# A one-element exponential after the gelus of seven of the nine first MLP stages, and fills dealt 12, 10, 9 instead of 14, 9, 8

## The chip, the cores and the metric

The kernel runs on one core of a Trainium2 chip. The metric is the device time of one execution in microseconds (us), median over several runs. A profile is one execution, and its span (first to last instruction) is some 2 us shorter than the time. All runs told of here count as fast, with a granted TensorE clock of 0.998 to 1.000 but for four long ones.

Names: PE is TensorE, ACT is ScalarE, DVE is VectorE, POOL is GpSimd. "L223" is line 223 of the kernel. The changed kernel has a few lines more, so that line 223 of before (exp of the scores) is line 228 after it, and 232 in two of the experiments.

## The reference

Forgetting attention over 8 batches, 8 heads, 576 tokens, 64 per head, and then an MLP with the tanh form of gelu over all 4608 tokens:

```python
scores = scale * q @ k.T + (cum[:, None] - cum[None, :])   # cum: running sum of log f
attn   = softmax(causal(scores)) @ v
x      = attn as (4608, 512)
h      = x @ w_in                       # 512 -> 2048
out    = gelu_tanh(h) @ w_out           # 2048 -> 512
```

Two functions of ScalarE alternate, exp for the softmax and gelu for the MLP, and the engine loads a table at each change (seven loads for the gelus and seven for the exps of the scores in the steady part of the trace).

## The kernel before

The heads are worked in groups of four, `i` = 0 to 15, and the tokens in nine chunks of 512, `c`. A loop step does the first MLP stage of chunk `c` (eight pieces, a gelu behind each) and then a pair of head groups. In between it strews *fills*: `out_part(c, n)` issues `n` steps of the second MLP stage, so that PE has work while ACT turns scores into exponentials.

```python
def scores(i, r, groups=((0, 1, 2, 3),)):
    ...
        tiles = {g: psS.tile([128, 2, 512], FP32, name="ps_s", tag="s") for ...}   # both buffers of psS
        ...  matmuls of the four heads into the two tiles
        for g, t in tiles.items():
            nc.scalar.activation(p[:, 2 * g:2 * g + 2, off:off + n], t[:, :, 0:n], AF.Exp, scale=scale)   # L223

def mlp_in(c, prs):
    ...
        nc.scalar.activation(gT[c % 2][:, 2 * pr:2 * pr + 2, :], ph, AF.Gelu_apprx_tanh)   # L332

def pair(i, j, c):
    D, V = ...                           # D: denominators, V: attention output
    beside(i, 0, c, [D(j), 14])          # scores of round 0, D(j), masks of the round, 14 fills
    beside(i, 1, c, [V(j, 0), 9])
    beside(i, 2, c, [V(j, 1), 8])
    ...

run(FRONT)                               # an opening table of words (it holds chunks 0 and 1): S/H scores, F/f fills,
for c in range(2, NCH):                  # J/I first MLP stage, B idle matmuls, D, V, ...
    out_part(c - 1, CH)
    ...
    for pr in range(2, NP):
        mlp_in(c, (pr,))
    if c + 1 < B:
        out_part(c, 6)
        pair(2 * c + 3, 2 * c + 2, c)
```

A block of scores takes both buffers of `psS`; the next block can only start when both exps have read them. How many fills lie between two blocks decides whether PE gets there before ACT is done.

The softmax here doesn't subtract the row's maximum and nothing guards it: scores larger than these inputs give would overflow.

Of the kernel before, what the change touches and what calls it, by code (L numbers as in the profile page):

```python
# [8 lines left out]
FP32 = mybir.dt.float32  # L9
BF16 = mybir.dt.bfloat16  # L10
AF = mybir.ActivationFunctionType
# [5 lines left out]
def kernel(  # L17
# [10 lines left out]
    nc = tc.nc  # L28

    B, H, S, D = q.shape  # L30
# [44 lines left out]
        LP.3 B.1.256 vw.1.0 WI.1@LU.4 W H.1.1.1 WI.3 B.2.256 WI.2 H.1.0.0 M.1.0.1 D.0.0 M.1.0.0 H.0.1.1 V.0.0.0 H.0.1.0 B.2.256 M.0.1 H.1.1.0 V.0.1.0  # L75
        D.1.0 H.0.3.0 B.2.128 V.1.0.0 LX.1.1 H.0.3.1 V.1.1.0 m.0.3.2 H.1.3.0 m.0.3.4 B.1.256 VW.1.1 H.1.3.1 B.4.128 vw.0.1 D.0.1 M.1.3 S.1.2 M.1.1 LK.2
        V.0.1.1 V.0.0.1 WO.0 J.0.1 D.1.1 J.0.0 WO.1@LV.1.1 V.1.1.1 V.1.0.1 J.0.3 WO.2@WI.1 VW.3 J.1.0 WO.3 LK.3 LQ.3 J.1.1 TQ.2 J.1.3 LQ.4
        LX.1.0@WO.2 TK.2 J.0.2 J.1.2 LK.4 F.0.6 TK.3 B.3.256 S.2.0 LK.5 F.0.9 S.2.2 F.0.10 S.2.1 TQ.3 TQ.4 F.0.10 LV.2.0@LK.5 m.2.1 vw.2
        TK.4 S.3.0 f.0.1 M.2.2 CL.2 LQ.5 M.2.0 D.2 f.0.6 S.3.1 m.3.0 F.0.6 V.2.0 S.3.2 TK.5 LK.6 M.3.2 f.0.7 V.2.1 CL.3
        S.4.1 m.3.1 LQ.6 F.0.6 TQ.5 H.4.2.1 D.3 H.4.0.1 LQ.7 VW.4 H.4.0.0 V.3.1 v.3.0 f.0.3 H.4.2.0 CL.4 I.1.0 m.4.1 LV.2.1@LQ.5 I.1.5  # L80
        TQ.6 m.4.2.3 I.1.1 I.1.7 LV.3.0@LQ.7 m.4.2.2 TK.6 M.4.0 I.1.3 I.1.2 I.1.4 I.1.6 F.1.8 S.5.0 F.1.2 F.1.14 S.5.1 D.4 M.5.0 f.1.9
        S.5.2 V.4.0 m.5.2.3 f.1.6 VW.5 V.4.1 CL.5 m.5.2.2 LQ.8 S.6.0 f.1.6 M.5.1 D.5 f.1.4 S.6.1 V.5.1 f.1.7 V.5.0 vw.6 S.6.2
        m.6.1 M.6.2.2 m.6.0 m.6.2.3 LK.7 LK.8 CL.6 LX.3.1@LK.6
    """
# [1 line left out]
    singles = ctx.enter_context(tc.tile_pool(name="singles", bufs=1))  # L86
# [6 lines left out]
    def many(n, shape, dtype, name):  # L93
        return [singles.tile(shape, dtype, name=f"{name}{i}") for i in range(n)]
# [11 lines left out]
    vw = many(2, [128, NT + 1, 4, D], BF16, "vw")  # L106
# [9 lines left out]
    w_bf = singles.tile([128, NQ, NT + 1, 4], BF16, name="w_bf")  # L116
    shift = singles.tile([128, 1], FP32, name="shift")
    idle = singles.tile([128, 512], BF16, name="idle")
    causal = many(2, [128, 128], BF16, "causal")


# [62 lines left out]
    def key_columns(i, key, h, c):  # L184

        b0 = {"low": 0, 0: 1, 1: 3, 2: 5, 3: 7, "high": NB}[key]
        return kT[i % 2][32 * h:32 * h + 32, 64 * b0:64 * b0 + 128, c]

    idle_ps = []

# [6 lines left out]
    def scores(i, r, groups=((0, 1, 2, 3),)):  # L197

        qq, p = qT[i % 2], pt[i % 2]
        if i < 2:  # L200
            off, n = split_rounds[r]
            todo = [(key, col - off, q0, nq) for (key, col, q0, nq) in split_pieces[r]]
        else:
            off, n = rounds[r]
            todo = []
            for (key, col, q0, nq) in pieces:
                a, z = max(col, off), min(col + nq, off + n)
                if a < z:
                    todo.append((key, a - off, q0 + a - col, z - a))
        for heads in groups:  # L210
            tiles = {g: psS.tile([128, 2, 512], FP32, name="ps_s", tag="s") for g in sorted({h // 2 for h in heads})}
            for c in range(2):
                for j, (key, c0, q0, nq) in enumerate(todo):
                    for h in heads:
                        nc.tensor.matmul(  # L215
                            tiles[h // 2][:, h % 2, c0:c0 + nq],
                            key_columns(i, key, h, c),
                            qq[32 * h:32 * h + 32, q0:q0 + nq, c],
                            start=(c == 0 and j == 0), stop=(c == 1),
                            skip_group_check=True,  # L220
                        )
            for g, t in tiles.items():
                nc.scalar.activation(p[:, 2 * g:2 * g + 2, off:off + n], t[:, :, 0:n], AF.Exp, scale=scale)  # L223
# [68 lines left out]
    def denominators(i, part=None):  # L292

        def column(h):

            return lambda t: (w_bf[:, i, t, h:h + 1] if t not in (0, LOW) else
                              w_bf[:, i, t, h:h + 1].to_broadcast([128, 32]))

        po = product(i, [(32 * h, column(h), h) for h in range(4)], False, part)
        n = S if part is None else parts[part][1] - parts[part][0]  # L300
        den = den_pool.tile([128, S], FP32, name="den", tag="den")
        nc.vector.transpose(out=den[:, 0:n], in_=po)  # L302
        rec = den_pool.tile([128, S // 32], FP32, name="rec", tag="rec")
        nc.vector.reciprocal(rec[:, 0:n // 32], den[:, 0:n:32])
        rb = den_pool.tile([128, S], FP32, name="rb", tag="rb")
        nc.vector.transpose(out=rb[:, 0:n].rearrange("p (c j) -> p c j", j=32),  # L306
                            in_=rec[:, 0:n // 32].unsqueeze(2).to_broadcast([128, n // 32, 32]))
        rbs[i, part] = rb[:, 0:n]

    def attn_out(i, x, spare=False, part=None):  # L310
        b, u = i // QPB, i % QPB
        po = product(i, [(32 * h, lambda t, h=h: vw[i % 2][:, t, h, x:D:2], h) for h in range(4)], spare, part)
        s0, s1 = (0, S) if part is None else parts[part]
        nc.vector.tensor_mul(xT[:, 2 * u + x, S * b + s0:S * b + s1], po, rbs[i, part])  # L314
# [37 lines left out]
    def mlp_out(c):  # L352

        for n in range(CH // 128):
            r0 = CH * c + 128 * n
            last = c == NCH - 1 and n == CH // 128 - 1
            st = ostage_pool.tile([128, D_MODEL], FP32, name="o_st", tag="o")
            for (m0, m1) in ((0, 384), (384, 512)) if last else ((0, D_MODEL),):
                pso = psM.tile([128, D_MODEL], FP32, name="pso", tag="m")
                for ft in range(N_FT):  # L360
                    cols = 32 if by_columns else 128
                    for c0 in range(0, 128, cols):
                        nc.tensor.matmul(pso[c0:c0 + cols, m0:m1],  # L363
                                         gT[c % 2][:, ft, 128 * n + c0:128 * n + c0 + cols],
                                         w_out_sb[:, ft, m0:m1],
                                         start=(ft == 0), stop=(ft == N_FT - 1), skip_group_check=True)
                    if ft == N_FT - 1:
                        nc.vector.tensor_copy(st[:, m0:m1], pso[:, m0:m1])  # L368
                        eng = nc.scalar if m0 else nc.sync
                        eng.dma_start(out=out[r0:r0 + 128, m0:m1], in_=st[:, m0:m1])  # L370
                    yield
# [61 lines left out]
    def pull(it, n):  # L433
        for _ in range(n):
            if next(it, False) is False:
                return
# [4 lines left out]
    def out_part(c, n, tiled=0):  # L441
        by_columns[:] = [True] * tiled
        pull(fills.setdefault(c, mlp_out(c)), n)
# [5 lines left out]
    def load_values(b, half):  # L449
# [33 lines left out]
        "F": out_part,  # L483
        "f": lambda c, n: out_part(c, n, 1),
        "B": keep_busy,
    }

    def run(table):
# [10 lines left out]
    def beside(i, r, c, todo):  # L499

        if i is not None:
            scores(i, r)
        for n, x in enumerate(todo):
            if isinstance(x, int):
                out_part(c, x, 1)
            else:
                x()
            if n == 0 and i is not None:
                after_scores(i, r)

    def after_scores(i, r):
        mask(i, r)
        if r == 1:
            make_vw(i, nc.gpsimd)
        if r == 2:
            copy_low(i)

    def pair(i, j, c):

        D, V = (lambda q: lambda: denominators(q)), (lambda q, x, spare=False: lambda: attn_out(q, x, spare))  # L520
        beside(i, 0, c, [D(j), 14])
        beside(i, 1, c, [V(j, 0), 9])
        beside(i, 2, c, [V(j, 1), 8])
        if i + 1 < NQ:
            beside(i + 1, 0, c, [D(i), 10])
            beside(i + 1, 1, c, [V(i, 0), 5, V(i, 1), 4])
            scores(i + 1, 2)
            after_scores(i + 1, 2)
        else:
            beside(None, 0, c, [D(i), 10, V(i, 0), V(i, 1, True), 10])  # L530
# [11 lines left out]
    with tc.manual_schedule():  # L542
        setup()
        run(FRONT)
        for c in range(2, NCH):
            out_part(c - 1, CH)
            for pr in range(2):
                mlp_in(c, (pr,))
            if c + 1 < B:
                prepare(2 * c + 3, 2 * c + 4)  # L550
            if c + 2 < B:
                load_v(c + 2)
            for pr in range(2, NP):
                mlp_in(c, (pr,))
            if c + 1 < B:
                out_part(c, 6)
                pair(2 * c + 3, 2 * c + 2, c)
        out_part(NCH - 1, CH)
# [30 lines left out]
```

## Time and profile before

| | before |
|---|---|
| time, median of 6 runs | 343.32 us (342.74 to 343.62) |
| span of the profile | 341.2 us |
| opening, from the idle matmuls at 42.17 us to the first MLP stage of chunk 1 at 68.39 | 26.22 us, PE busy 24.98 |
| chunk 1, the rest of the opening table, 68.39 to 104.36 | 35.97 us, PE busy 35.97 |
| steps c = 2 to 6, 104.36 to 282.42 | 178.06 us, PE busy 177.78 |
| tail (c = 7 and 8), 282.42 to the end | 58.78 us |

The rows come from asking the busy time of each engine in those stretches, which start and end at the same instructions in every kernel here. I call 42.17 to 68.39 the *opening* and 68.39 to 282.42 (214.03 us) the *loop*, though its first 35.97 us belong to the opening table: they are the stage of chunk 1. What is not PE's busy time looks like what a change outside PE can win: 1.24 us in the opening, nothing in chunk 1, and 0.28 us after it.

Rows, in order of time: start, duration, engine, line, operation, count; in brackets the idle time before it and who ended it.

```profile
47.21 2.33 PE L363 MATMUL pso<-w_out_sb,gT 128*128 128x512 bf16 x10
...
64.20 1.14 PE L215 MATMUL ps_s<-qT,kT 32*128 32x64 bf16 x24
...
66.38 0.87 PE L283 MATMUL ps_o<-pt,vw 128*32 128x512 bf16 x24 [0.24 <-ACT pt L223]
...
275.00 0.28 PE L283 MATMUL po<-pt,w_bf 128*1 128x192 bf16 x8 [0.28 <-POOL pt L229]
```

and ACT:

```profile
65.31 1.94 ACT L223 ACTIVATE pt<-ps_s 128x1024 bf16<-128x1024 f32 x2 [0.70 <-PE ps_s L215]
```

From the start of a block of scores at 64.20 to its exps at 65.31 it takes 1.11 us. The row at 275.00 is the last pair's wait for a mask.

### The profile page before, as it was taken

How to read it: one execution, taken by the hardware profiler on the slowest of the kernel's cores; microseconds unless marked ns; L12 is line 12 of the kernel's file. 1: busy time of each engine (PE TensorE's matmuls, PEld its weight loads, DVE VectorE, ACT ScalarE, POOL GpSimd, SP SyncE). 2: the span in 40 equal slices, each digit the busy share in tenths (PEclk: the TensorE clock that was granted, in tenths of full speed). 3: DMA queues.
4: the chain of work that ended last, by engine and by line, in shares of the span. 5: the costliest groups of instructions: out<-in, count | busy, mean ns of one | idle time of the engine just before them, and what ended most of it. 6: DMA issues, size and time to landing. Idle time of an engine off the chain costs nothing.

```text
span 341.2 us, 9416 instructions
## 1 busy us (share of the span) xinstructions
PE 330.1 (97%) x4241; PEld 162.2 (48%) x4241; DVE 132.2 (39%) x206; ACT 191.3 (56%) x194; POOL 110.0 (32%) x155
## 2 busy tenths in 40 slices
PE   3999989999999999999999999999999999999996
PEld 1458834544454445444444444444444544444443
DVE  4785049740455435603452234414430450011011
ACT  4784576676557566656575665665575724502510
POOL 8996551600506224601651055105410410000000
PEclk9999999999999999999999999999999999999999
DMA  7999999670315971491029310920100011011012
GB/s 122 213 214 208 194 230 190 106 171 2 87 46 77 244 159 35 120 200 52 35 67 202 73 66 35 190 51 33 65 31 2 33 52 44 2 61 61 0 39 86
DMA packets 40200, 33.26 MB, mean 97 GB/s; under 512 B 27472, under 2 KB 29776, under 8 KB 40160
## 3 DMA queue, kind: packets, MB, share of 16 engines
q0 software_dynamic: 8848, 16.58, 27.5%
q1 hardware_dynamic: 31168, 16.01, 16.9%
q8 instruction: 33, 0.54, 0.7%
q10 hardware_dynamic: 144, 0.07, 0.1%
q14 instruction: 7, 0.06, 0.1%
HBM read 36.85 MB, written 9.44 MB: 136 GB/s over the span
## 4 chain that ended last, share of the span: by engine, by line
PE 83%; POOL 1%; ACT 1%; issue 1%; POOLq 0%; DVE 0%; ACTq 0%
PE pso L363 35%; PE ps_h L325 32%; PE po L283 8%; PE ps_s L215 7%; ACT pt L223 1%; POOL vw L177 1%; PE ps_o L283 0%; POOL pt L229 0%; POOLq L584 0%; DVE o_st L368 0%; POOLq L229 0%; ACTq L223 0%
## 5 line engine op out<-in xcount | busy, mean ns | idle before, releaser
L363 PE MATMUL pso<-w_out_sb,gT 128*32 128x512 bf16 (+3 forms) x1492 | 134.5, 377 | 0.0
L223 ACT ACTIVATE pt<-ps_s 128x1024 bf16<-128x1024 f32 (+2 forms) x100 | 93.9, 991 | 49.6 <-PE ps_s L215 42.2
L325 PE MATMUL ps_h<-xT,w_in_sb 128*128 128x512 bf16 x512 | 111.9, 379 | 0.0
L332 ACT ACTIVATE gT<-ps_h 128x1024 bf16<-128x1024 f32 x64 | 65.5, 1023 | 64.2 <-PE ps_h L325 64.2
L229 POOL TENSOR_SCALAR_AFFINE_SELECT pt<-pt 128x512 bf16<-128x512 bf16 (+3 forms) x65 | 38.0, 594 | 141.6 <-ACT pt L223 140.8
L363 PEld LDWEIGHTS <-gT 128*32 128x32 bf16 (+1 forms) x1492 | 56.3, 97 | 56.8 <-issue 3.5
L325 PEld LDWEIGHTS <-w_in_sb 128*128 128x128 bf16 x512 | 50.0, 98 | 60.4 <-issue 0.4
L368 DVE COPY o_st<-pso 128x512 f32<-128x512 f32 (+2 forms) x37 | 24.9, 673 | 72.2 <-PE pso L363 71.8
L215 PE MATMUL ps_s<-qT,kT 32*128 32x64 bf16 (+5 forms) x896 | 36.3, 263 | 1.2 <-ACT pt L223 1.2
L302 DVE STREAM_TRANSPOSE den<-po 128x576 f32<-128x576 f32 x14 | 11.0, 783 | 64.5 <-PE po L283 64.5
L314 DVE TENSOR_TENSOR xT<-po,rb 128x576 bf16<-128x576 f32 x26 | 19.7, 757 | 32.7 <-PE po L283 32.6
L177 POOL TENSOR_TENSOR vw<-v_nat,wT 128x1280 bf16<-128x1280 f32 (+1 forms) x13 | 30.0, 2309 | 0.1
L215 PEld LDWEIGHTS <-kT 32*128 32x128 bf16 x896 | 16.6, 93 | 24.8 <-issue 19.4
L160 DVE STREAM_TRANSPOSE kT<-k_c 128x576 f32<-128x576 f32 x16 | 19.9, 1246 | 16.5 <-DMA k_c<-in_k_dram 16.5
L283 PE MATMUL po<-pt,vw 128*32 128x64 bf16 (+4 forms) x624 | 22.4, 278 | 0.0
L160 DVE STREAM_TRANSPOSE qT<-q_c 128x576 f32<-128x576 f32 x16 | 19.9, 1244 | 1.5 <-DMA q_c<-in_q_dram 0.8
L283 PEld LDWEIGHTS <-vw 128*32 128x32 bf16 x672 | 14.2, 97 | 12.2 <-issue 4.1
L131 POOL DMA_DIRECT2D v_nat<-in_v_dram x20 | 15.3, 777 | 3.6 <-DMA w_out_sb<-in_moe_w_out_dram 3.6
L342 PE MATMUL ps_h<-xT,w_in_sb 128*128 128x256 bf16 x128 | 14.5, 273 | 0.0
L342 PEld LDWEIGHTS <-w_in_sb 128*128 128x128 bf16 x128 | 12.3, 98 | 1.7
L306 DVE STREAM_TRANSPOSE rb<-rec 128x576 f32<-128x576 f32 (+2 forms) x18 | 12.8, 712 | 0.6
L283 PE MATMUL po<-pt,w_bf 128*32 128x512 bf16 (+3 forms) x336 | 12.3, 278 | 0.3 <-POOL pt L229 0.3
(60 smaller groups left out, 120.3 us busy)
## 6 DMA issues: line engine op xcount, KB each, us to landing
out_dram<-o_st SPq DMA_DIRECT2D x35, 256.0 KB, 2.0
k_c<-in_k_dram POOLq DMA_DIRECT2D x16, 288.0 KB, 6.2
q_c<-in_q_dram POOLq DMA_DIRECT2D x16, 288.0 KB, 7.2
v_nat<-in_v_dram SPq DMA_DIRECT2D x16, 256.0 KB, 8.6
w_in_sb<-in_moe_w_in_dram POOLq DMA_DIRECT2D x4, 512.0 KB, 9.6
w_out_sb<-in_moe_w_out_dram POOLq DMA_DIRECT2D x4, 512.0 KB, 7.6
v_nat<-in_v_dram SPq DMA_DIRECT2D x16, 128.0 KB, 3.1
v_nat<-in_v_dram POOLq DMA_DIRECT2D x13, 128.0 KB, 7.3
```

Source lines behind the costliest of these rows:

```text
L160: nc.vector.transpose(out=dst.rearrange("p s c -> p (s c)").bitcast(FP32) .rearrange("p (t a) -> p a t", a=S // 32), in_=src.rearrange("p ...
L177: eng.tensor_mul(vw[i % 2][:, t0:t1], vb[:, t0:t1, h0:h0 + 4, :], wT[:, i, t0:t1, :].unsqueeze(3).to_broadcast([128, t1 - t0, 4, D]))
L215: nc.tensor.matmul(tiles[h // 2][:, h % 2, c0:c0 + nq], key_columns(i, key, h, c), qq[32 * h:32 * h + 32, q0:q0 + nq, c], start=(c == 0 an ...
L223: nc.scalar.activation(p[:, 2 * g:2 * g + 2, off:off + n], t[:, :, 0:n], AF.Exp, scale=scale)
L229: nc.gpsimd.affine_select(out=x, in_=x, compare_op=ALU.is_ge, fill=0.0, base=0, pattern=pattern, channel_multiplier=-1)
L283: nc.tensor.matmul(po[r0:r0 + w.shape[-1], 448 + q0:448 + q0 + nq], w, p[:, h, col:col + nq], start=(key in (0, "low")), stop=(key in ("lo ...
L314: nc.vector.tensor_mul(xT[:, 2 * u + x, S * b + s0:S * b + s1], po, rbs[i, part])
L325: nc.tensor.matmul(ph[:, j, :], w_in_sb[:, dt, 128 * ft:128 * ft + 128], xT[:, dt, CH * c:CH * (c + 1)], start=(dt == 0), stop=(dt == N_DT ...
L332: nc.scalar.activation(gT[c % 2][:, 2 * pr:2 * pr + 2, :], ph, AF.Gelu_apprx_tanh)
L342: nc.tensor.matmul(ph[:, j // 2, QA * (j % 2):QA * (j % 2) + QA], w_in_sb[:, dt, 128 * ft:128 * ft + 128], xT[:, dt, n0:n0 + QA], start=(d ...
L363: nc.tensor.matmul(pso[c0:c0 + cols, m0:m1], gT[c % 2][:, ft, 128 * n + c0:128 * n + c0 + cols], w_out_sb[:, ft, m0:m1], start=(ft == 0), ...
L368: nc.vector.tensor_copy(st[:, m0:m1], pso[:, m0:m1])
```

## The change

The intent is to load the exp table while ACT waits for the scores anyhow: a one-element exp, which waits for nothing, is issued behind the last gelu, and the load comes with it. As the exps then end earlier, the first of three blocks needs fewer fills, and the 31 fills are dealt more evenly.

```diff
-        ... J.0.2 J.1.2 LK.4 F.0.6 TK.3 B.3.256 S.2.0 ...
+        ... J.0.2 J.1.2 X LK.4 F.0.6 TK.3 B.3.256 S.2.0 ...
-        ... I.1.4 I.1.6 F.1.8 S.5.0 ...
+        ... I.1.4 I.1.6 X F.1.8 S.5.0 ...
+    spare = singles.tile([1, 1], FP32, name="spare")
+    def load_exp():
+        nc.scalar.activation(spare, shift[0:1, :], AF.Exp)
+        "X": load_exp,
-        beside(i, 0, c, [D(j), 14])
-        beside(i, 1, c, [V(j, 0), 9])
-        beside(i, 2, c, [V(j, 1), 8])
+        beside(i, 0, c, [D(j), 12])
+        beside(i, 1, c, [V(j, 0), 10])
+        beside(i, 2, c, [V(j, 1), 9])
             if c + 1 < B:
+                load_exp()
                 out_part(c, 6)
```

That makes seven exponentials: two in the opening table (behind chunks 0 and 1) and five in the steps c = 2 to 6.

More of the change, by code (lines that the diff above doesn't have):

```diff
@@ L77 @@
         V.0.1.1 V.0.0.1 WO.0 J.0.1 D.1.1 J.0.0 WO.1@LV.1.1 V.1.1.1 V.1.0.1 J.0.3 WO.2@WI.1 VW.3 J.1.0 WO.3 LK.3 LQ.3 J.1.1 TQ.2 J.1.3 LQ.4
-        LX.1.0@WO.2 TK.2 J.0.2 J.1.2 LK.4 F.0.6 TK.3 B.3.256 S.2.0 LK.5 F.0.9 S.2.2 F.0.10 S.2.1 TQ.3 TQ.4 F.0.10 LV.2.0@LK.5 m.2.1 vw.2
+        LX.1.0@WO.2 TK.2 J.0.2 J.1.2 X LK.4 F.0.6 TK.3 B.3.256 S.2.0 LK.5 F.0.9 S.2.2 F.0.10 S.2.1 TQ.3 TQ.4 F.0.10 LV.2.0@LK.5 m.2.1 vw.2
         TK.4 S.3.0 f.0.1 M.2.2 CL.2 LQ.5 M.2.0 D.2 f.0.6 S.3.1 m.3.0 F.0.6 V.2.0 S.3.2 TK.5 LK.6 M.3.2 f.0.7 V.2.1 CL.3
         S.4.1 m.3.1 LQ.6 F.0.6 TQ.5 H.4.2.1 D.3 H.4.0.1 LQ.7 VW.4 H.4.0.0 V.3.1 v.3.0 f.0.3 H.4.2.0 CL.4 I.1.0 m.4.1 LV.2.1@LQ.5 I.1.5
-        TQ.6 m.4.2.3 I.1.1 I.1.7 LV.3.0@LQ.7 m.4.2.2 TK.6 M.4.0 I.1.3 I.1.2 I.1.4 I.1.6 F.1.8 S.5.0 F.1.2 F.1.14 S.5.1 D.4 M.5.0 f.1.9
+        TQ.6 m.4.2.3 I.1.1 I.1.7 LV.3.0@LQ.7 m.4.2.2 TK.6 M.4.0 I.1.3 I.1.2 I.1.4 I.1.6 X F.1.8 S.5.0 F.1.2 F.1.14 S.5.1 D.4 M.5.0 f.1.9
         S.5.2 V.4.0 m.5.2.3 f.1.6 VW.5 V.4.1 CL.5 m.5.2.2 LQ.8 S.6.0 f.1.6 M.5.1 D.5 f.1.4 S.6.1 V.5.1 f.1.7 V.5.0 vw.6 S.6.2
```

## The prediction

> **What bounds the kernel now.** I read the page first (busy shares, the 40 slices, the chain that ended last), then what each engine waited for, then the order in time around each place that the change touches.
>
> ```profile
> PE 330.1 (97%) x4241; PEld 162.2 (48%) x4241; DVE 132.2 (39%) x206; ACT 191.3 (56%) x194; POOL 110.0 (32%) x155
> PE   3999989999999999999999999999999999999996
> PE 83%; POOL 1%; ACT 1%; issue 1%; POOLq 0%; DVE 0%; ACTq 0%
> ```
>
> TensorE (PE) is busy for 330.1 of the span's 341.2 us. The row of slices puts most of the missing 11 us into the first slice and the last one, before data arrive and while the last rows are written; the change touches neither. So a change of ScalarE's (ACT's) work can only pay where PE stands still for ACT, or for something that ACT releases. The list of PE's waits is short:
>
> ```profile
> PE ps_lt L397 <- POOL utri_f masks.py:66: 4.8, 1, 4.8
> PE ps_s L215 <- ACT pt L223: 1.2, 3, 0.6
> PE cum_ps L424 <- POOL before L417: 1.0, 1, 1.0
> PE po L283 <- POOL pt L229: 0.3, 1, 0.3
> PE ps_o L283 <- ACT pt L223: 0.2, 1, 0.2
> PE po_m L269 <- DVE pt L258: 0.2, 1, 0.2
> ```
>
> (Columns: total us, times, longest.) The 4.8 and the 1.0 lie in the set-up. What can be had from earlier exponentials is at most 1.2 + 0.3 + 0.2 = 1.7 us of 341.2, that is 0.5%.
>
> Now the table loads. ScalarE's groups by shape hold seven loads in front of exps of the scores (line 223), 1283 ns each, and the idle time before them is 6.1 us, all for the scores:
>
> ```profile
> L223 ACT ACT_TABLE_LOAD x7 | 9.0, 1283 | 6.1 <-PE ps_s L215 6.1
> L332 ACT ACT_TABLE_LOAD x7 | 9.0, 1283 | 0.1
> ```
>
> The loads for the gelus (line 332) don't wait: 0.1 us idle. Those for the exps come after the wait for the scores, so the load stands between scores and exp. These are the seven places that the change treats (two in the opening table, five in the loop, for c = 2 to 6).
>
> **What the Trainium skill says.** "ScalarE: Activation LUTs", section "What ACT_TABLE_LOAD costs", gives about 1283 ns for a load plus about 1380 ns of drain for each switch. The trace agrees with the 1283 exactly, and not with the drain: a load at 43.37 us is followed by its exp at 44.66, 1.29 later, and the gelus' load of 69.54 by its gelu at 70.83. I count 1.29 us per switch. The same section puts an ACTIVATE without pointer operands at 186 ns + 0.833 ns per element, with some 93 ns of overlap back to back; the 1024-element exps measure 1021 ns where that gives 1039, and two of them 1.94 us where 2 x 1.021 is 2.04, so the overlap is there. A one-element exp is then an estimate of 0.1 to 0.2 us. "Perfetto Trace Analysis", section "Identifying Dependency Chains", says that an instruction that waits on several engines may get EventSemaphore instructions ahead of it with the further waits. That explains the 6.1 us: the trace has 76 semaphore instructions of line 223 on ACT's queue, and a load placed directly before the exp sits behind them. "TensorE: Matmul & The Clock Gate", section "Wait — 56ns, not 53.3ns?", gives 215.7 ns for a warm matmul of 512 columns. The chain of waits has 14 fills (56 matmuls of 32 rows, four side by side) in 3.02 us: 215.7 ns a fill. So PE runs dry nowhere inside the fills.
>
> **Part one: the exponential.** It writes a tile of its own and reads a constant written at the start, so it waits for nothing; its load starts when the last gelu ends. It adds seven ACTIVATEs, about 7 x 0.2 = 1.4 us of ACT, an engine at 56%. The number of loads stays at seven for the exps; they move.
>
> Steady stage (c = 5), ACT then PE:
>
> ```profile
> 226.12 1.02 ACT L332 ACTIVATE gT<-ps_h 128x1024 bf16<-128x1024 f32 x1 [0.70 <-PE ps_h L325]
> 228.11 1.28 ACT L223 ACT_TABLE_LOAD   x1 [0.97 <-PE ps_s L215]
> 229.41 1.94 ACT L223 ACTIVATE pt<-ps_s 128x1024 bf16<-128x1024 f32 x2
> ...
> 228.62 3.20 PE L363 MATMUL pso<-w_out_sb,gT 128*32 128x512 bf16 x56
> 231.75 0.64 PE L215 MATMUL ps_s<-qT,kT 32*128 32x64 bf16 x16
> ```
>
> The last gelu ends at 227.14. The load would run from 227.15 to 228.43, the small exp to about 228.6, and the first real exp starts there instead of at 229.41: 0.8 us earlier. But both exps already end at 229.41 + 1.94 = 231.35, and PE, which needs the two score buffers back, comes for them at 231.75, after its 14 fills. The 0.4 us of slack becomes 1.2 and PE gains nothing. The stages from 104.52 on last 35.91, 35.92, 35.92 and 35.90 us with PE busy for all of it. So for c = 3, 4 and 5: zero. The stage of c = 2 needs no earlier load at all: there the load started at 83.51, straight after the gelu, and was over when the scores ended at 84.78; the small exp delays the first exp by some 0.2 us, and the next scores come only at 88.3, so again zero.
>
> The first of the seven is different:
>
> ```profile
> 42.59 0.69 PE L215 MATMUL ps_s<-qT,kT 32*128 32x64 bf16 x24
> 43.22 2.12 PE L363 MATMUL pso<-w_out_sb,gT 128*128 128x512 bf16 x9
> 45.74 0.32 PE L215 MATMUL ps_s<-qT,kT 32*128 32x320 bf16 x2 [0.40 <-ACT pt L223]
> 46.65 0.63 PE L215 MATMUL ps_s<-qT,kT 32*128 32x320 bf16 x14 [0.60 <-ACT pt L223]
> ```
>
> Only nine fills lie between these two blocks of scores, and PE stands 0.40 + 0.60 = 1.0 us for exps that started at 44.66 and ended at 46.60. The gelu before ends at 42.10; load to 43.39, small exp to 43.55 or so, real exps from about 43.6 to 45.5. PE resumes at about 45.6 instead of 46.65: 1.0 us off, with a rest of the wait of 0.1 to 0.3 us. From 46.65 on the chain that ended last is nearly all PE, and in this part of the trace ACT's exps again wait for PE, so the microsecond is carried to the end unless something tied to a transfer takes it up. **Gain: 1.0 us.**
>
> **Part two: 12, 10, 9 fills instead of 14, 9, 8.** Both sum to 31; at the end of three blocks PE stands where it stood. Blocks two and three start 2 and 1 fills earlier, 0.43 and 0.22 us. That needs part one: scores at 231.75 - 0.43 = 231.3 would meet exps ending at 231.35; with part one they end at 230.55. It moves the exps of rounds 1 and 2 earlier by 0.43 and 0.22 us, and so the masks on GpSimd. In the last pair (i = 15) this matters: the denominators wait there 0.28 us, at 275.00, for the mask of round 2, which ran from 273.73 after an exp that ended at 273.66. 0.22 us earlier leaves 0.06 of it. **Gain: 0.2 us.** Elsewhere such a mask ends just in time (it starts at 237.81 and takes 1.22; the denominators run from 238.77 to 239.64), so those get safer, not faster.
>
> Sum: 1.0 + 0.2 = 1.2 us off, 343.42 to 342.2.
>
> **Rivals.** (1) *Each switch is on the path*: seven times 0.8 to 1.29 us, 6 to 9 us, some 335 to 338. For it: the 6.1 us idle before the loads. Against it: PE's total wait for ACT is 1.4 us, and six of the seven places show none. (2) *The microsecond at 46 us is lost again*: a new wait of VectorE for the keys of a later head group (issued at 44.72, and such loads take 4.5 to 8.8 us to land, so 49 to 53.5; VectorE transposes them at 54.15, or 53.1 after the change), or of PE for the transposes. For it: that the transfers don't move with PE. Against: VectorE is not on the chain, and it waited for no transfer between 45 and 68 us. This would make 342.5 to 343.3. (3) *Even dealing makes a new wait*: if the small exp cost much more than 0.2 us, block two would wait for score buffers, up to 0.4 us in each of five stages, 344 to 345. Against: 0.8 us of slack by the working above. (4) *The fills' evictions* shift by one to three fills against the products; but VectorE is at 39%, and each pair of blocks still shares two buffers in the same order: under 0.3 us either way.
>
> **Range and chances.** The main term rests on one place that can be read directly; rival 2 can halve it, and repeats differ by 0.4 us. I take 342.2, with 341.5 to 343.3. Over 2% faster would be below 336.6, four times what PE's waits hold: 0.01. Slower by 2% needs 7 us of new waits: 0.01.
>
> **What would show it.** Right: seven loads for exps with next to no idle time put down to the scores before them; PE's wait at 45.7 us down from 1.0 to about 0.2; first exps 0.8 us earlier in the steady stages with the stage lengths still 35.9 us; the 0.28 us wait of the last denominators nearly gone. Wrong: stage lengths that change by more than 0.2 us, a new wait for score buffers in the second block of a pair, or PE's later time unmoved although it resumed earlier at 45.6.

## The result and the profile after

The changed kernel takes 341.48 us (median of 6 runs, 341.21 to 342.0) against 343.32. The ratio is 0.9949, 95% interval 0.9937 to 0.9962: faster by half a per cent. Ratios here are the mean time of one kernel's fast runs over that of the other's of the same rounds, so not quite the ratio of the medians quoted.

The page of the changed kernel (busy shares; the chain that ended last):

```profile
PE 329.8 (97%) x4241; PEld 162.0 (48%) x4241; DVE 132.3 (39%) x206; ACT 191.8 (56%) x201; POOL 110.1 (32%) x155
PE 90%; DMA 2%; POOL 2%; ACT 2%; DVE 1%; issue 1%; POOLq 0%; DVEq 0%; ACTq 0%
```

ACT has its seven instructions more (201 against 194). The chain before could be followed back only to 45.69 us, where PE had stood waiting for an exp; it now runs on through the opening's first MLP stage to the set-up, which is why PE's share rose from 83 to 90%: the wait that broke it is gone. ACT's groups by shape:

```profile
L192 ACT ACT_TABLE_LOAD x7 | 9.0, 1283 | 0.1
L192 ACT ACTIVATE spare<-shift 1x1 f32<-1x1 f32 x7 | 1.4, 202 | 0.1
```

The seven loads belong to the small exps (line 192) and no longer wait: 0.1 us of idle time in front of them where 6.1 stood. A small exp takes 202 ns.

The place in the opening, PE and then ACT:

```profile
43.00 0.70 PE L220 MATMUL ps_s<-qT,kT 32*128 32x64 bf16 x24
43.63 2.12 PE L368 MATMUL pso<-w_out_sb,gT 128*128 128x512 bf16 x9
45.68 0.83 PE L220 MATMUL ps_s<-qT,kT 32*128 32x320 bf16 x16
46.44 2.33 PE L368 MATMUL pso<-w_out_sb,gT 128*128 128x512 bf16 x10
```

```profile
42.53 1.28 ACT L192 ACT_TABLE_LOAD   x1
43.82 0.20 ACT L192 ACTIVATE spare<-shift 1x1 f32<-1x1 f32 x1
43.93 1.90 ACT L228 ACTIVATE pt<-ps_s 128x1024 bf16<-128x1024 f32 x2
```

From the start of the first block of scores to the fills behind the second it now takes 46.44 - 43.00 = 3.44 us. Before it took 47.21 - 42.59 = 4.62 (the row at 47.21, ten fills, is shown above). That is 1.18 us off. The second block has no wait in front of it; it takes 0.83 us, 0.20 more than an undisturbed block's 0.63, which is the rest of the wait.

The steady step c = 5, ACT:

```profile
226.06 1.28 ACT L192 ACT_TABLE_LOAD   x1
227.36 0.20 ACT L192 ACTIVATE spare<-shift 1x1 f32<-1x1 f32 x1
227.47 1.90 ACT L228 ACTIVATE pt<-ps_s 128x1024 bf16<-128x1024 f32 x2
230.95 1.94 ACT L228 ACTIVATE pt<-ps_s 128x1024 bf16<-128x1024 f32 x2 [1.58 <-PE ps_s L220]
```

The load sits against the last gelu, and the first exp comes 1.43 us after that gelu ends (226.04) instead of 2.27 (229.41 - 227.14). It buys only idle time: ACT waits 1.58 us for the next scores where it waited 1.14.

Then the rows that answer to the exp at 65.31 us ("the hiccup"): the exp comes 0.79 us after its scores started at 63.43 (1.11 before):

```profile
63.43 1.14 PE L220 MATMUL ps_s<-qT,kT 32*128 32x64 bf16 x24
64.22 1.94 ACT L228 ACTIVATE pt<-ps_s 128x1024 bf16<-128x1024 f32 x2 [0.39 <-PE ps_s L220]
```

And the last pair's denominators, in one piece of 24 where before a wait of 0.28 us parted them:

```profile
272.86 1.12 PE L288 MATMUL po<-pt,w_bf 128*32 128x512 bf16 x24
```

By stretches, the opening before and then after (length, then PE's busy time and matmuls; the rest of the row is other engines):

```profile
42.17:68.39 26.22, 24.98 (x426) 11.68 (x424) 19.08 (x26) 17.81 (x18) 12.19 (x19) 1.00 0.89 175
42.58:67.30 24.72, 24.72 (x425) 11.59 (x424) 18.98 (x26) 17.84 (x19) 11.36 (x17) 1.00 0.89 179
```

The opening takes 24.72 us instead of 26.22 (1.50 off), chunk 1 again 35.97, steps 2 to 6 177.84 instead of 178.06 (0.22 off), the tail 58.79 instead of 58.78. Together 1.71 us, against 1.75 by the ratio (0.0051 x 343.3). The spans differ by only 1.3 us because in this one profile the opening began 0.41 us later (42.58 against 42.17); over all the profiles told of here that point lies between 42.05 and 42.76 us, with no relation to the change.

So the gain has three pieces: 1.18 us at the first exponential, 0.31 us at the hiccup, 0.22 us in the last pair.

### The profile page after: what moved, and what is told of

The parts are those of the page before. It is cut to its first block, busy times and chain, and to the rows that moved or that the text cites. A ratio compares the mean times of both kernels' runs of the same rounds, so it can differ in the third digit from the quotient of the medians.

```text
span 339.9 us, 9423 instructions
## 1 busy us (share of the span) xinstructions
PE 329.8 (97%) x4241; PEld 162.0 (48%) x4241; DVE 132.3 (39%) x206; ACT 191.8 (56%) x201; POOL 110.1 (32%) x155
## 4 chain that ended last, share of the span: by engine, by line
PE 90%; DMA 2%; POOL 2%; ACT 2%; DVE 1%; issue 1%; POOLq 0%; DVEq 0%; ACTq 0%
PE pso L368 36%; PE ps_h L330 33%; PE po L288 8%; PE ps_s L220 8%; PE ps_h L347 4%; DMA v_nat<-in_v_dram 2%; ACT pt L228 2%; PE po_m L274 1%; POOL vw L178 1%; POOL v_nat L132 0%; PE ps_o L288 0%; DVE pt L263 0%; DVE vw L178 0%; POOL pt L234 0%; POOL q_c L155 0%
## 5 line engine op out<-in xcount | busy, mean ns | idle before, releaser
L155 POOL DMA_DIRECT2D k_c<-in_k_dram x16 | 9.1, 568 | 11.3 <-DVE kT L161 5.7
```

## The experiments

The theory to be tested: of the seven places only the first had PE waiting behind it, and the rest of the gain is the last pair's mask. Its rival: each of seven switches is worth the same, about 0.25 us. A second rival: the dealing pays. Single times spread by 0.5 us and more and the intervals are 0.15 to 0.4% wide on either side, so pieces of 0.2 to 0.3 us are read from the lengths of the stretches, which repeat within 0.02 us:

| kernel | opening, us | loop, us | median, us | median before, same rounds |
|---|---|---|---|---|
| before | 26.22 | 214.03 | | |
| changed | 24.72 | 213.81 | 341.48 | 343.32 |
| first_only | 24.71 | 214.02 | 341.70 | 343.20 |
| rest_with_deal | 26.21 | 213.81 | 342.93 | 343.20 |
| exp_no_deal | 24.72 | 214.02 | 341.54 | 343.20 |
| deal_only | 26.22 | 214.17 | 343.33 | 343.20 |
| copy_first | 25.91 | 214.03 | 342.67 | 343.24 |
| copy_late | 25.90 | 214.02 | 342.87 | 343.24 |
| last_deal_only | 26.21 | 213.88 | 343.03 | 343.24 |

All outputs are right. Five ratios below lie 0.0002 to 0.0012 under the ranges that were expected, chiefly because one long run of before (344.8 us in the rounds of first_only to deal_only, 347.34 in those of the last three) lifts before's mean. By medians four of the five lie inside; copy_first, at 0.9983, is 0.0002 under.

**first_only**: the first exponential alone.

```diff
-        ... I.1.6 X F.1.8 ...          (and load_exp() in the loop)
+        ... I.1.6 F.1.8 ...            (none in the loop; fills 14, 9, 8)
```

> Only the first of the seven exponentials (the one in the opening table, ahead of the scores at 42.6 us), fills dealt as before. Theory (only this place had a tensor-engine wait behind it): 1.2 us off in the profile between the fills that start at 47.21 us and the start of the run, plus, if the 0.3 us hiccup at 65 us goes with it as it did in the changed kernel, 1.5 us; so a time of 341.8 to 342.2, ratio 0.9955 to 0.9965. Rival (each of seven switches is worth the same): a seventh of 1.75 us, that is 0.25 us, ratio 0.9993.

Ratio 0.9952 (0.9938 to 0.9967). The opening takes 24.71 us: the whole 1.5 us comes from one of seven exponentials. The rival's 0.9993 is outside the interval.

**rest_with_deal**: the other six, with the dealing.

```diff
-        ... J.1.2 X LK.4 ...
+        ... J.1.2 LK.4 ...
```

> The other six exponentials and the even dealing, without the first. Theory: the 1.0 us wait at 45.7 us stays, only the last pair's wait of 0.28 us for its mask shrinks by 0.2; 0.2 us off, ratio 0.9990 to 1.0000. Rival (each switch is worth the same): six sevenths of 1.75 us, 1.5 us off, ratio 0.9956.

Ratio 0.9990 (0.9973 to 1.0006). In PE's order of time both parts of the wait are back:

```profile
46.01 0.32 PE L220 MATMUL ps_s<-qT,kT 32*128 32x320 bf16 x2 [0.40 <-ACT pt L228]
46.92 0.63 PE L220 MATMUL ps_s<-qT,kT 32*128 32x320 bf16 x14 [0.60 <-ACT pt L228]
```

The loop has its 0.22 us. Six exponentials together buy nothing that the loop's length shows beyond what the dealing explains, as the next two runs tell.

**exp_no_deal**: all seven exponentials, fills 14, 9, 8.

```diff
-        beside(i, 0, c, [D(j), 12])   ... 10, 9
+        beside(i, 0, c, [D(j), 14])   ... 9, 8
```

> All seven exponentials, fills dealt 14, 9, 8 as before. Theory: as the changed kernel but for the last pair: its wait of 0.28 us for the mask stays, so 1.5 us off, ratio 0.9950 to 0.9965; the stages of the loop still last 35.9 us. Rival (the dealing is what pays, in five stages): under half of the gain, ratio over 0.9975.

Ratio 0.9947 (0.9933 to 0.9962), loop 214.02 us. The five exponentials of steps 2 to 6 and the second of the opening table are worth 0.01 us by themselves. The last pair waits its 0.28 us again.

**deal_only**: fills 12, 10, 9, no exponential.

```diff
-        ... J.1.2 X LK.4 ... I.1.6 X F.1.8 ...
+        ... J.1.2 LK.4 ... I.1.6 F.1.8 ...
-                load_exp()
```

> Fills dealt 12, 10, 9 without any early exponential. Theory: the scores of the second block come at 231.75 - 0.43 = 231.32 us, when the exps end at 231.35 plus some 0.05, so a wait of 0.05 to 0.15 us in each of five stages that moves everything behind it; the last pair's mask wait still shrinks. 0.2 us faster to 0.6 us slower, ratio 0.9994 to 1.0018. Rival (dealing is good by itself): 1 us or more off, ratio under 0.997.

Ratio 1.0016 (0.9984 to 1.0047), lifted by one run of 346.78 us at a clock of 0.985; by time nothing is told apart. The loop takes 214.17 us, 0.36 more than with the exponentials (213.81), or 0.07 for each of the five steps c = 2 to 6. At c = 5 the second block of scores is where it goes:

```profile
229.42 2.76 PE L368 MATMUL pso<-w_out_sb,gT 128*32 128x512 bf16 x48
232.12 0.71 PE L220 MATMUL ps_s<-qT,kT 32*128 32x64 bf16 x16
```

It takes 0.71 us where it took 0.64: PE arrives after 12 fills and finds the exps, which end at 230.21 + 1.94 = 232.15, just unfinished. So the dealing needs the exponentials, and those of the loop pay through it alone.

**last_deal_only**: the dealing in the last pair only, no exponential.

```diff
-        beside(i, 0, c, [D(j), 12])   ... 10, 9
+        beside(i, 0, c, [D(j), 12 if i == 15 else 14])   ... 10 if i == 15 else 9, 9 if i == 15 else 8
```

> No early exponential, and 12, 10, 9 in the last pair alone. Theory: the last pair's wait of 0.28 us for the mask goes (0.22 us off), less the 0.07 us that dealing without the exponential cost per stage in the kernel with the dealing alone: 214.03 us between the start of the third chunk's first MLP stage and that of the last but one become 213.88. Below what times can show: ratio 0.9985 to 1.0010.

Ratio 0.9983 (0.9943 to 1.0022). The loop takes 213.88 us, the expected figure: 0.22 won at the mask, 0.07 lost at the second block.

**copy_first**: a placebo. A one-element copy, which brought no table load (the trace has as many as before's), takes the first exponential's place.

```diff
-        nc.scalar.activation(spare, shift[0:1, :], AF.Exp)     # X, first place
+        nc.scalar.copy(spare, shift[0:1, :])                   # K, the same place; no other part of the change
```

> A placebo for the first exponential: a one-element copy by ScalarE in its very place, which needs no table, so that the load stays behind the wait for the scores. Nothing else of the change. Theory (it is the moved load that pays): the wait of 1.0 us (0.40 + 0.60) at about 46 us stays. The hiccup of 0.3 us near 65 us, which so far went away in every kernel with the first exponential and stayed in every kernel without it: if it hangs on where ScalarE's instructions lie in the stream, one more instruction takes it away here too, so 0.3 us off, ratio 0.9985 to 1.0000; if it hangs on the earlier timing, it stays, ratio 0.9995 to 1.0010. Rival to the theory (any small instruction there wakes ScalarE up or shortens the way to the exps): 1.2 us or more off, ratio under 0.9970.

Ratio 0.9973 (0.9937 to 1.0008), which doesn't exclude the rival's "under 0.9970"; the profile does:

```profile
45.77 0.32 PE L224 MATMUL ps_s<-qT,kT 32*128 32x320 bf16 x2 [0.40 <-ACT pt L232]
46.69 0.63 PE L224 MATMUL ps_s<-qT,kT 32*128 32x320 bf16 x14 [0.60 <-ACT pt L232]
```

The wait of 0.40 + 0.60 us stays, so it is the moved load that wins the 1.18 us. But the opening takes 25.91 us, 0.31 less than before: the hiccup is gone.

**copy_late**: the same copy, 10 us later on ACT (at 52.28 us instead of 42.03; the "6 us" was a slip).

```diff
-        ... S.2.1 TQ.3 TQ.4 ...
+        ... S.2.1 K TQ.3 TQ.4 ...
```

> The same one-element copy alone, but placed on ScalarE some 6 us later, behind the exps of the scores that start at 49.5 us, where ScalarE then idles for 1 us. The wait of 1.0 us at 46 us stays. The hiccup near 65 us: gone if it hangs on the number of ScalarE's instructions ahead of it (the delay from the start of that block of scores to the exp falls from 1.11 to 0.79 us), still 1.11 if it hangs on when things run. Time 0 to 0.3 us off, ratio 0.9985 to 1.0005.

Ratio 0.9979 (0.9943 to 1.0015). The row of the hiccup:

```profile
65.30 1.94 ACT L232 ACTIVATE pt<-ps_s 128x1024 bf16<-128x1024 f32 x2 [0.39 <-PE ps_s L224]
```

Its scores started at 64.51, so 0.79 us again, and the opening takes 25.90. In the four kernels in which no instruction was added to ACT ahead of this point (before, rest_with_deal, deal_only, last_deal_only) it is 1.09 to 1.11 us, and in the others 0.79, wherever the extra instruction lay and whether or not the load moved. Six exponentials behind that point (rest_with_deal) don't take it away. So the 0.31 us hang on one more ACT instruction lying ahead, not on the earlier exps; why is open. The traces narrow it down. It is no late wait: in before, PE's signal for this exp came at 64.91, GpSimd's last one at 61.98, ACT's semaphore instruction just ahead was at 64.93, and the exp followed only at 65.31; in copy_late the same two stand at 65.24 and 65.30. And it goes with the fetching of instructions: a packet of 8192 bytes of the kind "instruction" on DMA queue 14 starts 3.05 to 3.31 us after this exp in the four kernels with the hiccup, and 0.49 to 1.28 us after it in the eight profiles without. The packet comes after the pause, so it is not shown to make it.

**after_again** and **no_idle, no_idle_again**: a step further. In the opening ACT's chain (last gelu, load, small exp, two exps) now sets when the second block may start, and PE spends 0.43 us of that time on three idle matmuls. They are dropped, and real fills pulled forward.

```diff
-        ... TK.3 B.3.256 S.2.0 LK.5 F.0.9 S.2.2 F.0.10 S.2.1 TQ.3 TQ.4 F.0.10 LV.2.0 ... D.2 f.0.6 S.3.1 ...
+        ... TK.3 S.2.0 LK.5 F.0.12 S.2.2 F.0.9 S.2.1 TQ.3 TQ.4 F.0.9 LV.2.0 ... D.2 f.0.5 S.3.1 ...
```

> The changed kernel, further: the three idle matmuls ahead of the first exponential's scores are dropped, and the fills near there dealt 12, 9, 9, then 5, instead of 9, 10, 10, then 6. Theory: ScalarE's chain (last gelu, load, exponential, two exps) sets when the second block of scores may start, some 0.2 us after PE comes for it; work that PE can do until then is free. 0.43 us of idle matmuls go and 0.2 us of waiting is filled, so 0.4 to 0.65 us better than the changed kernel: 340.8 to 341.1, ratio to the kernel before 0.9925 to 0.9945. Rival (fills taken from later blocks make new waits there): no better than the changed kernel, ratio 0.9945 to 0.9955.

> The changed kernel itself, unedited, beside the next run and on the same chip, so that the two can be compared. Expected as before: 341.2 to 341.8, ratio 0.994 to 0.996.

> The same kernel as no_idle. Its profile says 0.37 us better than the changed kernel (25.65 against 26.02 us from the first fills after the first MLP stage's gelus to the next MLP stage). If that is real, the ratio to the kernel before is 0.0011 below that of the changed kernel in these rounds, 0.993 to 0.995; if the fills taken from later blocks cost as much elsewhere, the two ratios agree within 0.0003.

no_idle: median 341.10, ratio 0.9936 (0.9896 to 0.9976). In the later rounds no_idle_again has 341.08, ratio 0.9936 (0.9901 to 0.9971), beside the changed kernel's 341.75, ratio 0.9967 (0.9923 to 1.001). One run of the changed kernel there, at 345.46 us, lifts its ratio; the medians are 0.67 us apart. PE in no_idle_again:

```profile
42.54 0.69 PE L220 MATMUL ps_s<-qT,kT 32*128 32x64 bf16 x24
43.16 2.76 PE L368 MATMUL pso<-w_out_sb,gT 128*128 128x512 bf16 x12
45.86 0.63 PE L220 MATMUL ps_s<-qT,kT 32*128 32x320 bf16 x16
```

The second block takes its plain 0.63 us after twelve fills instead of nine. From the fills ahead of the first block to the loop it is 25.65 us in one profile and 25.63 in the other, against 26.02 in both profiles of the changed kernel (41.28 to 67.30, 41.22 to 67.24); the loop is 213.80. So 0.37 to 0.39 us repeat, a little under the expected 0.4 to 0.65: part is lost again in blocks that now come after fewer fills (the third takes 0.73 us in place of 0.64). Against the changed kernel this rests on the stretches and medians; the two ratios' intervals overlap.

## Why the prediction was right

The prediction of 342.2 us (341.5 to 343.3) stands beside a measured 341.48, 0.02 us below the lower end of its range; by the ratio and the prediction's own starting point (343.42, one of the six runs of before), 0.9949 x 343.42 = 341.67, inside it. The mechanism was right, its sum of 1.2 us was too small by half a microsecond.

**What bounds the kernel.** Right. But that the cap of 1.7 us met the measured 1.71 is luck. Of the 1.2 us that PE waited for exps of the scores, 0.2 lie at 13.76 us, in the set-up, and are there after the change too; the waits that the change could reach sum to 1.0 + 0.3 + 0.2 = 1.5. The other 0.2 us lie in what the list counts as busy: the opening's busy time fell by 0.26 us. ACT's own list would have misled: its 6.1 us of idle time in front of the loads shrank to 0.1 and paid 1.18 us.

**Why a load waits.** The prediction took the load to sit behind semaphore instructions. A listing of the compiled kernel says the same more plainly: the load holds one of its exp's waits, and which one that is decides what the load waits for.

```
before, first place    LoadActFuncSet [waits PE]     Activation pt [waits Pool]
before, second place   LoadActFuncSet [waits DVE]    Activation pt [waits PE]
changed, first place   LoadActFuncSet                Activation spare     Activation pt [waits PE,Pool]
```

The traces agree with it: the semaphore instruction ahead of the load waits for PE's signal in the first place (at 43.32 us, the load at 43.37) and for VectorE's in the second (at 82.47). VectorE was long done, and the load ran at 83.51, straight behind the gelu, without any change; in the changed kernel none stands ahead of the load at 42.53. This second place is chunk 1's, in the opening table; the prediction calls it the stage of c = 2, and its stages "c = 3, 4 and 5", from 104.52 us on, are c = 2 to 5. Nothing in its sum depends on the names.

**Part one, first place: 1.0 us.** Right in kind, and the term was mis-sized: 1.18 us measured. The prediction put the exps' start at "about 43.6", 1.01 us after the scores' start at 42.59; it is 0.93 us after it (43.93 - 43.00), because the small exp overlaps the next by 0.09 us (43.82 + 0.20 against 43.93). Against 2.07 us before (44.66 - 42.59) that is 1.14 us earlier, and the two exps take 1.90 us in place of 1.94: together the 1.18. The remaining tenth was rounding, of the exps' end to 45.5, of PE's start to 45.6 and of the gain to 1.0. first_only shows that this place alone carries the opening's whole gain, and copy_first that the wait stays where the load stays.

**Part one, steady stages: zero.** Right. The exps come 0.84 us earlier against the last gelu (0.8 predicted), and exp_no_deal's loop lasts 214.02 us against 214.03. In the second place the small exp delayed the first exp by 0.10 us rather than 0.2, which nothing waits for.

**Part two: 0.2 us.** Right: 0.22 us, in rest_with_deal, in the changed kernel and, less 0.07, in last_deal_only. That the dealing needs part one is shown by deal_only.

**The step that failed** is the sum, 0.51 us too small: 0.18 of that is the first place's term, 0.02 the dealing's, and 0.31 the hiccup near 65 us, for which it has no term. The prediction wrote that "in this part of the trace ACT's exps again wait for PE", so that the microsecond would be carried through unchanged. It was carried through, but one of those exps also started 0.3 us later than its scores explained, and one more ACT instruction ahead of it, exp or copy, ends that. It was in plain sight, as 0.36 us of "issue" in the chain of waits and in PE's 0.24 us of waiting for ps_o, which I counted into the cap and not into the sum. The copies show that it isn't the table's doing; its cause is not settled. That its size doesn't depend on when things run (0.30 to 0.32 us, in four kernels at 65.31 to 65.90 us) and the shifted instruction packets speak for something in ACT's instruction stream, but no run shows what.

**The rivals.** Every switch on the path: refuted by first_only and rest_with_deal. The microsecond lost again to a transfer: it was not, the stretches behind it are as long as before. A new wait from the dealing: real, but only without the exponentials, 0.07 us a step. Evictions: nothing seen, the loop is the same to 0.02 us.

## What to carry to other kernels

Count what the bound engine waits for before counting what the other engine loses: moving six of the seven table loads won 0.01 us by itself here. A load is worth moving where too little other work lies behind it, and putting more of that work there can win some more, as the version without idle matmuls shows (0.37 to 0.39 us); whether it could replace the exponential was not tried. A placebo in the place of the new instruction tells a moved cost from a shifted instruction stream, and stretches between fixed instructions resolve 0.1 us where times over whole runs don't resolve 0.5.

## What the Trainium skill lacked or had wrong

- "ScalarE: Activation LUTs", section "What ACT_TABLE_LOAD costs": its load of about 1283 ns is right to the nanosecond, but its drain of about 1380 ns for each switch is not in this trace; in the changed kernel a gelu ends at 226.04, the load runs from 226.06 and the exp starts at 227.36, so a switch costs 1.3 us, and the page's budget of about 2.66 us is twice too high here.
- The same page, section "Step-by-step: what each stage is for", says that the load is placed right before the ACTIVATE that needs it, and not that the load can then stand behind one of its semaphore waits: 6.1 us of ScalarE idle in front of seven loads, 0.1 us once a one-element ACTIVATE that waits for nothing led the way. No page names that remedy.
- Section "What ACT_TABLE_LOAD costs" has 186 ns + 0.833 ns per element, which gives an estimate of 187 ns for one element; 202 ns were measured, 0.09 us of which overlaps the next instruction as the section says.
- No page has the hiccup: an exp that started 0.3 us later than its scores allowed (1.09 to 1.11 us after the scores' start, against 0.79) until one more ScalarE instruction lay ahead of it.
